# A fused adaLN block on one core: output weights padded by the host, one double tile for the copied heads, the quad's turn two units behind its addition, and other filler rates

## The chip, the cores and the metric

The kernel runs on one core of a Trainium2 chip. The metric is the device time of one execution in microseconds (us). Times are compared as medians over runs; a profiled execution gives one further time and the trace behind every row shown here. The engines are called PE (matrix products), ACT, DVE, POOL and SP; SP issues nearly all DMAs, in its program's order.

## The reference

One transformer block over x of 2048 rows by 448 columns, in float32 (16 heads of 28 columns, a causal sliding window of 256):

```python
mod = (_silu(c) @ w_mod).reshape(c.shape[0], 6, 1, -1)
sa, ca, ga, sb, cb, gb = ...
h = _layernorm(x) * (1 + ca) + sa
x = x + ga * attention(h, wqkv, wo)      # softmax(q k^T * 28**-0.5, window 256) v, then @ wo
h = _layernorm(x) * (1 + cb) + sb
x = x + gb * (mish(h @ w1 + b1) @ w2)    # w1: 448 x 1792, w2: 1792 x 448
```

## The kernel before

**Precision.** Each float32 factor is split into a high part (rounded to the type that PE takes at full rate) and a low part, the difference. A product is made of three passes (high-high, high-low, low-high). For the probabilities, ACT writes the exponential twice (`P` exact, line 733, `Ph` rounded, line 734), and POOL subtracts them (`Pl`, line 741).

**Stages.** The 2048 rows form four groups of 512. A start-up stage normalises group 0 and makes its first projections. Then comes the attention loop, and behind it the two products with w1 and w2 (the feed-forward part, lines 938 and 1124 to 1126), in which PE alone decides.

**The attention loop.** It runs over 64 *slots* (group, head), each of three *units*; u counts units, 48 to a group, and v = u - 48 g is a unit's number within its group. All engines work through their own instructions in the order in which the loop wrote them. In a unit the loop writes, in this order:

- `PV(u-4, Pl)`, the product of low probabilities and values; in the first unit of a slot, `EV` copies a finished head out of PSUM on ACT (line 757);
- `B(u)`: the score product (line 719) and mask (line 730) on PE, then the two exponentials;
- `SP(u-1)`: the subtraction on POOL;
- `A`: three slots ahead, a score product (line 689) whose row maximum DVE takes (line 691). Two PSUM banks serve these;
- in every second slot `M2`: the maxima of two heads are transposed on PE into a corner of the last of those banks (line 697), DVE reads it out as `mr` (lines 699 and 700), and SP copies `mr` into two extra rows of the query tiles (`q<-mr`), so that `B` subtracts the maximum by itself. `B` of those heads waits for that copy; the next but one `A` product waits for DVE to have read the corner, since it reuses the bank;
- the steps of the *quad* (below), a share of *filler*, and `PV(u-2, Ph)`.

**The quad.** `EV` leaves a head as 60 rows in `O2`: 32 of high part (28 of output, one of denominator, three of zero), then 28 of low part. A single `O2` tile has room for two heads, one in either half. `EM`, one unit later, copies both parts with two DMAs into four-head tiles `O4` and `OL4` (`o<-t` with 32 rows, `ol<-t` with 28 rows). When four heads are there, four steps follow in four units, from u = 20 + 12 qd on: `QA` adds the tiles on POOL (line 777), `T1` transposes 32x32 blocks on DVE and takes the reciprocal of the denominators (lines 783, 785), `TM` multiplies on POOL (line 790), `T2` transposes back on DVE (line 794). After the fourth quad a group's attention output is full.

**Filler.** In between, PE makes the products that other groups need: in group g the last query and key tiles of g (`qk_5`, `qk_2`, `qk_6`), then, once the output of group g-1 is full, the products with wo of group g-1 (`wo`), then transposes and projections of group g+1 (`tr`, `qk`, `qk_v`). `RATE[g]` credits are added per unit, `FRONT[g]` units at double rate, and pieces are taken while credit lasts. `load_slot` forces what a coming slot needs, so that in unit 34 of a group a large piece runs at once. A side generator loads and prepares weights; its DMAs stand in a list `later` and are issued one at a time.

**wo.** In group 0 the side generator loads wo: four tiles `wop`, each zeroed on POOL (line 575) and filled by four DMAs of 28 rows (`wo_load`, four heads of 28 rows at a spacing of 32). It then multiplies them by the gate and splits them.

Of the kernel before, what the change touches and what calls it, by code (L numbers as in the profile page):

```python
# [51 lines left out]
def adaln_block(ctx: ExitStack, tc: tile.TileContext, x, wqkv, wo, w1, b1, w2, c, w_mod, out):  # L52
    nc = tc.nc
    PE, ACT, DVE, POOL = nc.tensor, nc.scalar, nc.vector, nc.gpsimd
# [3 lines left out]
    def dma(o, i):  # L58
        nc.sync.dma_start(o, i)

    def pool(name, side="left", space=None):
        kw = {} if space is None else {"space": space}
        cm = tc.tile_pool(name=name, bufs=1, reuse_waits="tile", side=side, **kw)
        st = ExitStack()
        return st.enter_context(cm), st
# [25 lines left out]
    def bank(tag, bufs, name):  # L91
        return PS[0].tile([128, 512], F32, name=name, tag=tag, bufs=bufs)
# [18 lines left out]
    for k in range(4):  # L111
        wmf = st0.tile([128, 2 * D], F32, name=f"wm01_{k}")
        t = wmf[0:112]
# [217 lines left out]
    later = []  # L331
# [190 lines left out]
    att, att_s = pool("att")  # L522
# [1 line left out]
    Q3 = [Q2[i // 2][:, i % 2] for i in range(NQ)]  # L524
    k3_tile(att, NK - 1)

    O4, OL4, (T4, O2) = [[att.tile([128, GT], F32, name=f"{n}_{i}") for i in range(2)] for n in ("o4", "ol4", "t4")]
    for t in OL4:
        POOL.memset(t, 0.0)
    wo3 = [mid.tile([128, D], F32R, name=f"wo3_{i}", tag="wo", bufs=8) for i in range(4)]  # L530
    wol = [mid.tile([128, D], F32R, name=f"wol_{i}", tag="wo", bufs=8) for i in range(4)]

# [11 lines left out]
    def gen_wm_sum(i, pl):  # L544
        ws = []
        for k in range(4):
            wm_load(i, k, pl, ws)
            yield
        yield
        yield  # L550
        flush()
        for k in range(4):
            yield "dve"
            mod_sum(k, ws[k], ws[0])
        yield
        return ws[0]

    def gen_mod_wo():
        acc = yield from gen_wm_sum(2, qk)
        yield "bank"  # L560
        p = bank("mm", 2, "ga")
        PE.matmul(p[:, 0:D], ones, acc, start=True, stop=True)
        ga = xr_tile("ga")[:, 0:D]
        ACT.activation(ga, p[:, 0:D], AF.Copy)
        pieces = []

        def wo_load(ci, t):
            for a in range(4):
                r = (4 * ci + a) * DH
                dma(t[32 * a:32 * a + DH], wo[r:r + DH, :])  # L570

        for ci in range(4):
            t = stg(qk, f"wop{ci}")
            pieces.append(t)
            POOL.memset(t, 0.0)
            later.append(lambda ci=ci, t=t: wo_load(ci, t))
            yield
        yield
        flush()
        for ci in range(4):  # L580
            w = pieces[ci]
            POOL.tensor_tensor(w, w, ga, op=ALU.mult)
            yield "act"
            split_hi(w, wo3[ci], ACT)
            yield "dve"
            split_lo(w, wo3[ci], wol[ci], 0, DVE)
            yield
# [87 lines left out]
    NS = NG * H  # L675
    mx, Pt, Ph, Pl, pvb = {}, {}, {}, {}, {}
# [59 lines left out]
    def SP(u):  # L736
        i, b = divmod(u, 3)
        c0 = units(i // H, b)[0][3]
        Pl[u] = att.tile([128, 512], F32R, name=f"Pl{u}", tag="Pl", bufs=4)
        for eng, a, b in ((POOL, c0, 512),) if u < NU - 5 else ((POOL, 0, 256), (DVE, 256, 512)):  # L740
            eng.tensor_tensor(Pl[u][:, a:b], Pt[u][:, a:b], Ph[u][:, a:b].bitcast(F32), op=ALU.subtract)  # L741
# [12 lines left out]
    def EV(i):  # L754
        a, b, n = i % 4 * 32, i % 2 * 64, i // 4 % 2
        if i < NS - 4:
            ACT.activation(O2[b:b + 60], pvb[i][0:60, :], AF.Copy)
        else:
            ACT.activation(O4[n][a:a + 32], pvb[i][0:32, :], AF.Copy)
            DVE.tensor_copy(OL4[n][a:a + DH], pvb[i][32:60, :])  # L760

    def EM(i):
        a, b, n = i % 4 * 32, i % 2 * 64, i // 4 % 2
        if i < NS - 4:
            dma(O4[n][a:a + 32], O2[b:b + 32])
            dma(OL4[n][a:a + DH], O2[b + 32:b + 60])

    def quad(qd):
        g, ci = divmod(qd, 4)
# [4 lines left out]
    def QA(qd):  # L774
        o, t = quad(qd)
        for eng, a, b in ((POOL, 0, GT),) if qd < NS // 4 - 1 else ((POOL, 0, 192), (DVE, 192, GT)):
            eng.tensor_tensor(o[:, a:b], O4[qd % 2][:, a:b], OL4[qd % 2][:, a:b], op=ALU.add)

    rcq = {}

# [221 lines left out]
            told[g] = next(side[g], None)  # L1002

    RATE = {0: 0.62, 1: 0.97, 2: 0.97, 3: 0.65}
    FRONT = {0: 0, 1: 2, 2: 2, 3: 2}
    ln1 = {g: gen_ln1(g) for g in range(1, NG)}
    fillers = {g: fill_main(g) for g in range(NG)}
# [2 lines left out]
    def step(g):  # L1010
        return next(fillers[g], 99.0) or RATE[g]

# [29 lines left out]
    for i in range(LEAD):  # L1042
# [4 lines left out]
        if i % 2:  # L1047
            M2(i // 2, "A")
            load_slot(LEAD + 1)
    NU = 3 * NS  # L1050
    credit = 0.0
    for u in range(NU + 9):
        s, k = divmod(u, 3)
        g = s // H
        if k == 0 and s % H == 0 and 0 < g < NG:
            drain(fillers[g - 1], side[g - 1])
            flush()
        pipe.step()
        if 0 <= u - 4 < NU:
            PV(u - 4, Pl)  # L1060
            if k == 0:
                EV(s - 2)
        if u < NU:
            B(u)
        if 0 <= u - 1 < NU:
            SP(u - 1)
        a = s + LEAD
        if a < NS:
            A(a, (0, 1, 3)[k])
        if k == s % 2 and s < NS:  # L1070
            load_slot(s + LEAD + 2)
        qd, w = divmod(u - 20, 12)
        if 0 <= qd < NS // 4 - 1 and w < 4:
            (QA, T1, TM, T2)[w](qd)
        if k == 0 and s - 2 == NS - 1:
            for f in (QA, T1, TM, T2):
                f(NS // 4 - 1)
        if g < NG:
            v = u - 48 * g
            if v in (0, 12):  # L1080
                chunk["v"] = 4 if v == 0 and g or 0 < g < NG - 1 else 2
            if v == 0:
                credit = 0.0
            credit += RATE[g] * (2 if v < FRONT[g] else 1)
            while credit > 0.0:
                credit -= step(g)
        if k == 0 and (a - 1) % 2 == 1 and LEAD <= a - 1 < NS:
            M2((a - 1) // 2)
        if g < NG:
            if v > 1 or g == 0:  # L1090
                side_step(g, ("dve", "act")[a >= NS:] if k == 1 else ("act",) if k == 0 and s % 2 == 0 else ())
            if later and ((s + (k == 2)) % 2 == 0 or k == 1):
                later.pop(0)()
        if k == 1 and 0 <= s - 2:
# [65 lines left out]
    for n in range(NN + 1):  # L1160
        g, f = divmod(n, NF)
# [44 lines left out]
```

## Time and profile before

| quantity | value |
|---|---|
| median of 3 runs (lowest, highest) | 742.61 us (738.5, 749.46) |
| the profiled execution | 740.08 us, its span 738.3 us |
| PE busy | 690.1 us, 93% of the span |
| DVE, ACT, POOL busy | 395.3, 391.5, 348.6 us |
| mean granted clock of PE | 0.98 |
| chain that ended last | PE 30%, of it most in lines 938 and 1124 to 1126 |

The page takes the span from the first to the last instruction; 1.8 us of the execution lie outside it. The attention loop's first exponential starts at 47.8 us and its last group at 347.8 us; from about 450 us on PE is busy without a break. Rows of a timeline give start, duration, engine, line and operation, and in square brackets how long the engine stood idle before and what ended that. "PEclk" is the clock that PE was granted, 1.00 being full speed.

### The profile page before, as it was taken

The page shows a single profiled execution, that of the slowest core. Times are in us where ns is not written, and L with a number is a line of the kernel's source. Part 1 is how long each engine was busy: PE and PEld are TensorE (multiplying, and loading weights), DVE is VectorE, ACT ScalarE, POOL GpSimd, SP SyncE. Part 2 cuts the span into 40 slices and gives each one's busy share as a digit, 9 for nine tenths or more (in the row PEclk, how much of TensorE's full clock was granted, in tenths as well). Part 3 has the DMA queues.
Part 4 walks back from the last instruction along what each step waited for, and adds up shares of the span by engine and source line. Part 5 has one row for each costly group of instructions (what it writes and reads, how often), then busy time and mean ns, then how long its engine had stood idle before and what let it go on. Part 6 is the DMA issues. An engine that isn't in the chain of part 4 may idle for free. (4 is left out here: it accounts for less than half of the span.)

```text
span 738.3 us, 12000 instructions
## 1 busy us (share of the span) xinstructions
PE 690.1 (93%) x3873; PEld 585.9 (79%) x3873; DVE 395.3 (54%) x993; ACT 391.5 (53%) x723; POOL 348.6 (47%) x364
## 2 busy tenths in 40 slices
PE   8999888889999979999979789999999999999996
PEld 7777667668887858888768678888888888888885
DVE  5677654667856677846658886333323232413112
ACT  4568565568846677856767795334224223322221
POOL 6536585678656688737678967432010000000002
PEclk9999998989999999999999999999999999999999
DMA  7856764265566374485676338410200020001001
GB/s 215 263 189 208 223 187 144 63 203 158 168 187 203 109 217 148 120 233 160 195 223 186 92 87 273 135 38 0 101 1 1 0 100 1 0 1 51 0 1 50
DMA packets 53730, 91.13 MB, mean 123 GB/s; under 512 B 8086, under 2 KB 28228, under 8 KB 53668
## 3 DMA queue, kind: packets, MB, share of 16 engines
q1 hardware_dynamic: 53204, 90.36, 40.0%
q8 instruction: 31, 0.51, 0.3%
q14 instruction: 31, 0.25, 0.1%
q10 hardware_dynamic: 464, 0.00, 0.0%
HBM read 53.34 MB, written 29.36 MB: 112 GB/s over the span
## 5 line engine op out<-in xcount | busy, mean ns | idle before, releaser
L741 POOL TENSOR_TENSOR Pl<-P,Ph 128x512 fp32r<-128x512 f32 (+2 forms) x192 | 232.3, 1217 | 105.7 <-ACT Ph L734 69.2
L691 DVE CUSTOM_DVE_ANT_0 junk<-sA,mask 128x384 bf16<-128x384 f32 (+2 forms) x256 | 135.2, 528 | 104.2 <-PE sA L689 93.0
L733 ACT ACTIVATE P<-sB 128x512 f32<-128x512 f32 (+2 forms) x192 | 109.6, 571 | 81.8 <-PE sB L730 74.8
L946 DVE TENSOR_TENSOR al<-t,ah 128x512 fp32r<-128x512 f32 x56 | 40.0, 714 | 187.3 <-ACT ah L945 187.3
L944 ACT ACTIVATE t<-z,b1c 128x512 f32<-128x512 f32 x56 | 38.5, 687 | 188.9 <-PE z L938 185.7
L689 PE MATMUL sA<-k,q 84*128 84x384 f32 (+2 forms) x256 | 103.4, 408 | 19.8 <-DVE mr L700 10.5
L734 ACT ACTIVATE Ph<-sB 128x512 fp32r<-128x512 f32 (+2 forms) x192 | 109.4, 570 | 0.0
L719 PE MATMUL sB<-q,k 86*128 86x256 f32 (+1 forms) x352 | 77.7, 295 | 16.1 <-DMA q<-mr 13.5
L938 PE MATMUL z<-hhf,w 128*128 128x512 f32 x224 | 89.5, 399 | 0.0
L938 PE MATMUL z<-hlf,w 128*128 128x512 f32 x224 | 88.5, 395 | 0.0
L1124 PE MATMUL acc<-w2h,ah 128*128 128x448 f32 x224 | 81.9, 366 | 0.0
L1126 PE MATMUL acc<-w2h,al 128*128 128x448 f32 x224 | 81.8, 365 | 0.0
L1125 PE MATMUL acc<-w2l,ah 128*128 128x448 f32 x224 | 81.6, 364 | 0.0
L751 PE MATMUL pv<-Ph,v 128*60 128x256 f32 (+2 forms) x352 | 79.8, 302 | 0.0
L719 PEld LDWEIGHTS sB<-q,k 86*128 86x128 f32 x352 | 62.1, 195 | 21.4 <-issue 10.8
L751 PE MATMUL pv<-Pl,v 128*60 128x256 f32 (+2 forms) x352 | 75.6, 289 | 0.1
L689 PEld LDWEIGHTS sA<-k,q 84*128 84x128 f32 x256 | 50.4, 199 | 30.5 <-DVE mx L691 14.1
L938 PE MATMUL z<-hhf,w1l 128*128 128x512 f32 x168 | 66.4, 395 | 0.0
L730 PE MATMUL sB<-fdmask,identr 128*128 128x128 bf16 (+1 forms) x320 | 61.6, 259 | 0.0
L751 PEld LDWEIGHTS pv<-Ph,v 128*60 128x60 f32 x352 | 47.2, 137 | 12.9 <-issue 0.6
L1133 POOL TENSOR_TENSOR yo<-yo,x 128x448 f32<-128x448 f32 (+1 forms) x4 | 4.2, 1058 | 108.1 <-DVE yo L1130 108.1
L751 PEld LDWEIGHTS pv<-Pl,v 128*60 128x60 f32 x352 | 47.1, 136 | 7.8 <-POOL Pl L741 0.4
(157 smaller groups left out, 1289.3 us busy)
## 6 DMA issues: line engine op xcount, KB each, us to landing
scr<-st SPq DMA_DIRECT2D x24, 512.0 KB
k<-scr SPq DMA_DIRECT2D x48, 252.0 KB
q<-scr SPq DMA_DIRECT2D x64, 168.0 KB
scr<-st SPq DMA_DIRECT2D x32, 256.0 KB
x<-x1d SPq DMA_DIRECT2D x10, 448.0 KB
o<-t SPq DMA_DIRECT2D x60, 64.0 KB
xin<-in_A_x_dram SPq DMA_DIRECT2D x8, 448.0 KB
xr<-in_A_x_dram SPq DMA_DIRECT2D x16, 224.0 KB
```

The lines of the kernel that those rows point to most:

```text
L689: PE.matmul(p[:, c0:384], q[0:84, t * 128:(t + 1) * 128], k[0:84, t * 128 + c0:t * 128 + 384], start=True, stop=True)
L691: DVE.tensor_tensor_reduce(out=junk[:, c0:384], in0=p[:, c0:384], in1=mask[:, c0:384], scale=1.0, scalar=-3.0e38, op0=ALU.add, op1=ALU.max ...
L719: PE.matmul(p[:, c:c + 128 * (t1 - t0)], k[:, jj * 128:(jj + 1) * 128], q[:, t0 * 128:t1 * 128], start=(n == 0), stop=False, skip_group_ch ...
L730: PE.matmul(p[:, c:c + n], identr, fdmask[:, m:m + n], start=False, stop=True, skip_group_check=True)
L733: ACT.activation(P[:, c0:], p[:, c0:], AF.Exp, scale=SCALE)
L734: ACT.activation(Ph[u][:, c0:], p[:, c0:], AF.Exp, scale=SCALE)
L741: eng.tensor_tensor(Pl[u][:, a:b], Pt[u][:, a:b], Ph[u][:, a:b].bitcast(F32), op=ALU.subtract)
L751: PE.matmul(pv[0:60, t0 * 128:t1 * 128], V[j % NV][:, h, :], P[u][:, c:c + 128 * (t1 - t0)], start=(P is Ph and b == 0 and n == 0), stop=F ...
L938: PE.matmul(zb[n], ps[m][1], ps[m][0], start=(m == 0), stop=(m == 10))
L1124: PE.matmul(p, ah[n][:, ts], w2h[f], start=(f == 0), stop=False)
L1125: PE.matmul(p, ah[n][:, ts], w2l[f], start=False, stop=False)
L1126: PE.matmul(p, al[n][:, ts], w2h[f], start=False, stop=(f == NF - 1))
```

## The change

- **wo from the host's layout.** The host pads wo from 16 x 28 rows to 16 x 32 rows with zeros. Each of the four tiles is then filled by one DMA of 128 rows; the four zeroing instructions on POOL and 12 of the 16 DMAs are gone.
- **Double tiles.** `O4` and `OL4` become one tile with two halves, `O4[n][:, 0]` and `O4[n][:, 1]`. Both copies of `EM` have 32 rows. `O2` becomes two tiles of two heads each, so that `EV(i)` reuses the place of head i-4 and not of head i-2.
- **The turn.** `QA`, `T1`, `TM` and `T2` stand in units 0, 2, 3 and 5 behind u = 20 + 12 qd, where they stood in 0, 1, 2 and 3.
- **Filler rates.** In the first 13 units of a group (behind `FRONT`) the rate is multiplied by 0.65 in groups 1 and 2 and by 0.8 in group 3; from unit 13 on by 1.15 in groups 1 to 3. Group 0 keeps its rate.

```diff
-    O4, OL4, (T4, O2) = [[att.tile([128, GT], F32, name=f"{n}_{i}") for i in range(2)] for n in ("o4", "ol4", "t4")]
-    for t in OL4:
+    O4 = [att.tile([128, 2, GT], F32, name=f"o4_{i}") for i in range(2)]
+    O2 = [att.tile([128, GT], F32, name=f"o2_{i}") for i in range(2)]
+    T4 = att.tile([128, GT], F32, name="t4")
+    for t in O2:
         POOL.memset(t, 0.0)
+    POOL.memset(O4[(NG * H // 4 - 1) % 2][:, 1], 0.0)
...
-        def wo_load(ci, t):
-            for a in range(4):
-                r = (4 * ci + a) * DH
-                dma(t[32 * a:32 * a + DH], wo[r:r + DH, :])
...
-            POOL.memset(t, 0.0)
-            later.append(lambda ci=ci, t=t: wo_load(ci, t))
+            later.append(lambda ci=ci, t=t: dma(t, wo[ci * 128:(ci + 1) * 128, :]))
...
-            ACT.activation(O2[b:b + 60], pvb[i][0:60, :], AF.Copy)
+            ACT.activation(O2[i // 2 % 2][b:b + 60], pvb[i][0:60, :], AF.Copy)
...
-            dma(O4[n][a:a + 32], O2[b:b + 32])
-            dma(OL4[n][a:a + DH], O2[b + 32:b + 60])
+            for j in range(2):
+                dma(O4[n][a:a + 32, j], O2[i // 2 % 2][b + 32 * j:b + 32 * j + 32])
...
+    LATE = {0: 1.0, 1: 1.15, 2: 1.15, 3: 1.15}
+    EARLY = {0: 1.0, 1: 0.65, 2: 0.65, 3: 0.8}
...
+    QSTEP = {0: QA, 2: T1, 3: TM, 5: T2}
...
-        if 0 <= qd < NS // 4 - 1 and w < 4:
-            (QA, T1, TM, T2)[w](qd)
+        if 0 <= qd < NS // 4 - 1 and w in QSTEP:
+            QSTEP[w](qd)
...
-            credit += RATE[g] * (2 if v < FRONT[g] else 1)
+            credit += RATE[g] * (2 if v < FRONT[g] else EARLY[g] if v < 13 else LATE[g])
...
+        if name == "A_wo":
+            a = _np.pad(a.reshape(H, DH, D), ((0, 0), (0, 32 - DH), (0, 0))).reshape(H * 32, D)
```

**DVE around the eighth quad's first transposition** (group 2, unit 9; `t` and `on` are the quad's tiles, `mr` the maxima read out, `junk,mx` a row maximum). Before:

```order
L691 ISA junk,mx_3551<-sA_0_3552,mask 128x384
L691 ISA mx_3551 128x1
L783 STREAM_TRANSPOSE t_0_466<-on_2426 128x512
L785 RECIPROCAL rc_3556<-t_0_466 128x16
L699 CAST mr_3559<-sA_3_3530 8x128
L700 TENSOR_TENSOR mr_3559<-sA_3_3530,mr_3559 8x128
L691 ISA junk,mx_3551<-sA_1_3578,mask 128x384
```

and now:

```order
L688 ISA junk,mx_3535<-sA_0_3536,mask 128x384
L688 ISA mx_3535 128x1
L696 CAST mr_3540<-sA_3_3514 8x128
L697 TENSOR_TENSOR mr_3540<-sA_3_3514,mr_3540 8x128
L688 ISA junk,mx_3535<-sA_1_3559,mask 128x384
L688 ISA mx_3535 128x1
L780 STREAM_TRANSPOSE t_466<-on_2404 128x512
L782 RECIPROCAL rc_3565<-t_466 128x16
```

The transposition and the reciprocal, which wait for `QA` on POOL, stood ahead of the two instructions that read the maxima out; they now stand behind these and behind one more row maximum. The same holds at every quad of the loop.

**SP in group 0, where wo is loaded** (`wop` are the tiles of wo, `scr<-st` a store of projected queries and keys, `q<-mr` the copy of the maxima). Before:

```order
L59 DMA wop_1361<-in_A_wo_dram 28x448 x4
L59 DMA wop_1393<-in_A_wo_dram 28x448 x4
L59 DMA o_0_462<-t_1_467 32x512
L59 DMA ol_0_464<-t_1_467 28x512
L59 DMA wop_1423<-in_A_wo_dram 28x448 x4
L59 DMA scr<-st_1_1392 128x2x512
L59 DMA scr<-st_1_1392 128x512
L59 DMA q_0_376<-mr_1511 1x8x128 x2
```

and now:

```order
L59 DMA wop_1360<-in_A_wo_dram 128x448
L59 DMA wop_1388<-in_A_wo_dram 128x448
L59 DMA o_0_462<-o_0_464 32x512 x2
L59 DMA wop_1417<-in_A_wo_dram 128x448
L59 DMA scr<-st_1_1387 128x2x512
L59 DMA scr<-st_1_1387 128x512
L59 DMA q_0_376<-mr_1492 1x8x128 x2
```

Ahead of this `q<-mr` stand nine DMAs fewer in these rows; three more are gone at the first `wop` tile, a few rows earlier. Both copies of a head now have 32 rows.

**PE's filler**, counted unit by unit in PE's order (too long to show): in groups 1 and 2 the tile `qk_6` ends in unit 5 before and in unit 6 now, and the products with wo start in unit 16 before and in unit 18 now, so that the run of units without filler is 6 to 15 before (ten) and 7 to 17 now (eleven). At a group's end it is 46 and 47 before and 45 to 47 now (with four transposed columns in one of them). The forced piece in unit 34 has 33 products before and 26 now. In group 3, `qk_6` ends in unit 8 before and in 10 now, and wo starts in 16 before and in 17 now, and ends in 30 in both. Group 0 is the same in both.

More of the change, by code (lines that the diff above doesn't have):

```diff
@@ L756, in EV @@
         if i < NS - 4:
-            ACT.activation(O2[b:b + 60], pvb[i][0:60, :], AF.Copy)
+            ACT.activation(O2[i // 2 % 2][b:b + 60], pvb[i][0:60, :], AF.Copy)
         else:
-            ACT.activation(O4[n][a:a + 32], pvb[i][0:32, :], AF.Copy)
-            DVE.tensor_copy(OL4[n][a:a + DH], pvb[i][32:60, :])
+            ACT.activation(O4[n][a:a + 32, 0], pvb[i][0:32, :], AF.Copy)
+            DVE.tensor_copy(O4[n][a:a + DH, 1], pvb[i][32:60, :])
     def EM(i):
@@ L776, in QA @@
         for eng, a, b in ((POOL, 0, GT),) if qd < NS // 4 - 1 else ((POOL, 0, 192), (DVE, 192, GT)):
-            eng.tensor_tensor(o[:, a:b], O4[qd % 2][:, a:b], OL4[qd % 2][:, a:b], op=ALU.add)
+            eng.tensor_tensor(o[:, a:b], O4[qd % 2][:, 0, a:b], O4[qd % 2][:, 1, a:b], op=ALU.add)
     rcq = {}
@@ L1196 @@
     for name in _INS:
-        a = _np.ascontiguousarray(inputs[name])
+        a = inputs[name]
+        if name == "A_wo":
+            a = _np.pad(a.reshape(H, DH, D), ((0, 0), (0, 32 - DH), (0, 0))).reshape(H * 32, D)
+        a = _np.ascontiguousarray(a)
         arrays[f"in_{name}_dram"] = a
```

## The prediction

> **What bounds the kernel now.** I began with the page: its busy line and, of the slices, PE and its clock (tenths of each fortieth of the span).
>
> ```profile
> PE 690.1 (93%) x3873; PEld 585.9 (79%) x3873; DVE 395.3 (54%) x993; ACT 391.5 (53%) x723; POOL 348.6 (47%) x364
> PE   8999888889999979999979789999999999999996
> PEclk9999998989999999999999999999999999999999
> ```
>
> The second half of the span, the feed-forward part, is full on PE, and no edit touches it. PE's gaps lie in the attention loop, some 50 to 450 us. Next I asked who waited for whom, in the loop's terms (us in all, times, longest).
>
> ```profile
> PE sB L719 <- DMA q<-mr: 13.5, 7, 5.7
> PE sA L689 <- DVE mr L700: 10.5, 7, 3.0
> PE sA L689 <- DVE mx L691: 8.2, 16, 1.1
> PE sB L719 <- ACT Ph L734: 2.3, 3, 1.3
> ACT t L757 <- DMA ol<-t: 11.1, 8, 3.0
> DVE t L783 <- POOL on L777: 6.1, 5, 2.1
> ```
>
> Both large PE waits are for the maxima: `sA` for their being read out of its bank, `sB` for their copy landing. DVE's wait for POOL (`t <- on`, T1 waiting for QA) is not PE's own, but what is queued behind T1 is that very read-out. The timeline shows it, DVE and PE in group 2:
>
> ```profile
> 262.87 0.08 DVE L691 DVE_READ_ACCUMULATOR2_ANT mx<- 128x1 f32 x1
> 265.08 0.71 DVE L783 STREAM_TRANSPOSE t<-on 128x512 f32<-128x512 f32 x1 [2.13 <-POOL on L777]
> 265.83 0.25 DVE L785 RECIPROCAL rc<-t 128x16 f32<-128x16 f32 x1
> 266.25 0.28 DVE L700 TENSOR_TENSOR mr<-sA,mr 8x128 fp32r<-8x128 f32 x1
> 266.58 0.45 PE L689 MATMUL sA<-k,q 84*128 84x384 f32 x1 [2.96 <-DVE mr L700]
> ...
> 158.39 0.71 DVE L783 STREAM_TRANSPOSE t<-on 128x512 f32<-128x512 f32 x1 [2.11 <-POOL on L777]
> 159.88 0.69 PE L689 MATMUL sA<-k,q 84*128 84x384 f32 x1 [2.94 <-DVE mr L700]
> ```
>
> DVE stood 2.1 us for QA, spent 1 us on the turn, then freed the bank. The same happens in group 1, at the same unit 9. The largest wait, 5.7 us, is for `q<-mr`; SP's queue before it:
>
> ```profile
> 101.98 3.43 SPq L59 DMA_DIRECT2D wop<-in_A_wo_dram  x8
> 105.51 0.56 SPq L59 DMA_DIRECT2D o<-t  x1
> 106.12 0.81 SPq L59 DMA_DIRECT2D ol<-t  x1
> 107.03 1.78 SPq L59 DMA_DIRECT2D wop<-in_A_wo_dram  x4
> 108.90 0.91 SPq L59 DMA_DIRECT2D scr<-st  x2
> 109.91 1.40 SPq L59 DMA_DIRECT2D q<-mr  x2
> ...
> 104.20 0.28 DVE L700 TENSOR_TENSOR mr<-sA,mr 8x128 fp32r<-8x128 f32 x1
> 112.84 0.66 PE L719 MATMUL sB<-q,k 86*128 86x384 f32 x1 [5.70 <-DMA q<-mr]
> ```
>
> The maxima were ready at 104.48 and issued at 109.91, behind twelve loads of wo. Last, stretches (length; busy and count of PE, weight load, DVE, ACT, POOL; granted clock; DMA share, GB/s): the two stalls, what follows each, the units without filler in groups 1 and 2 (units 6 to 15), and ten units with filler.
>
> ```profile
> 107.20:112.80 5.60, 0.00 (x0) 0.00 (x0) 1.76 (x2) 0.59 (x1) 2.74 (x3) 0.81 0.59 199
> 112.80:117.50 4.70, 4.66 (x17) 3.85 (x18) 0.74 (x5) 2.05 (x5) 1.73 (x2) 0.50 0.73 220
> 267.70:271.10 3.40, 3.40 (x18) 2.91 (x16) 1.96 (x8) 3.04 (x6) 3.36 (x4) 0.51 0.54 139
> 152.30:173.00 20.70, 16.25 (x97) 12.76 (x95) 14.33 (x41) 15.49 (x30) 16.90 (x19) 0.84 0.69 210
> 258.10:278.80 20.70, 16.31 (x104) 12.82 (x102) 15.33 (x43) 16.43 (x33) 17.45 (x20) 0.92 0.72 213
> 278.80:297.40 18.60, 18.60 (x127) 16.75 (x125) 12.70 (x40) 12.21 (x24) 15.23 (x14) 1.00 0.51 158
> ```
>
> With filler PE is full and decides. Without it nobody is full; POOL comes nearest. After each stall the clock is half for a few microseconds, which counts where PE decides.
>
> **The change part by part.** The sum is made against the profiled execution's 740.1 us, 2.5 under the median of 742.6.
>
> *Loads of wo.* Twelve of the sixteen issues go. By the rows above one takes 3.43/8 = 0.43 us, so the nine that stood in these rows give 3.9 us back; the three at the first tile, some 6 us earlier in an equally unbroken queue, give 1.3. What a load of 128 rows takes to issue no row shows; nearest are the gate's loads of 112 rows, and the copies of a head:
>
> ```profile
> L59 SPq DMA_DIRECT2D wm<-in_w_mod_dram x21: 363/432/1877, 1.8 to 349.3; - x21
> L59 SPq DMA_DIRECT2D o<-t x60: 548/564/1374, 59.1 to 425.9; - x60
> L59 SPq DMA_DIRECT2D ol<-t x60: 763/806/1448, 59.9 to 426.5; - x60
> L575 POOL MEMSET wop<- x4: 468/471/477, 93.4 to 98.8; 128x448 f32 x4
> ```
>
> So 0.43 as well (min/median/max in ns). `ol<-t` with 32 rows should cost `o<-t`'s 0.56, a quarter less than its 0.81. Then `q<-mr` is issued 5.4 us earlier, at 104.5, just when the maxima are there. It landed 112.84 - 109.91 = 2.9 us after its issue; so at 107.4, where PE began to wait at 112.84 - 5.70 = 107.14. Of the stall 0.3 stays: 5.4 gained. The half clock behind it costs half of 4.7 us, 2.35; it goes too. Together 7.75; I take 7. The low end is 3, if the landing and not the issue is what is late (the loads still bring their bytes, at a DMA share of 0.59 to 0.73). That a half clock follows is seen after 3.0 us of idleness (267.70: 0.51) as after 5.6. The Trainium skill (TensorE: Matmul & The Clock Gate, What's actually happening) puts the condition at an idle window of about 3.4 us; by that rule 2.35 would go as soon as the stall falls under 3.4, by the row only below 3. The row decides here; my 7 holds under both.
>
> *The turn.* T1 and the reciprocal leave the place ahead of the read-out: 10.5 us of PE waits can go at most. Of these 2.94 + 2.96 lie in the stretches without filler. There POOL limits what can come: 20.70 - 16.90 = 3.8 and 20.70 - 17.45 = 3.25 are all that POOL's own work leaves, so the two stalls fit, barely, 5.9 (low end 0, if POOL cannot run behind by the few buffers it has). The half clock there I count at nothing, since PE is not full. Of the remaining 4.6 I take 3.5. What is late next: T1 now stands ahead of a later maximum, for which PE's `sA` waits too. If it held PE at all 15 quads, that would be 15 x 0.96 = 14.4 us; but it stood ahead of maxima before as well, and two units cover QA (POOL: one subtraction and QA, some 2.5 us of about 4). I take 1. Net: 8.4 gained. T2, two units later than before, waits for nothing more; a group's output is full two units later, which is the filler's matter.
>
> *Two tiles for `O2`.* The 11.1 us that ACT waited go almost surely: its copy now waits for a DMA four heads back. What of it reaches PE is bounded by PE's wait for ACT, 2.3, and by 0 below; the 3.0 falls beside PE waiting for `q<-mr`, where nothing is gained. I take 1.5; the high end is 4, if the stretches without filler gain by it. The shorter second copy (0.24 x 60) is SP's time, counted above where it matters, elsewhere nothing: SP has room. Zeroing: four times 0.47 of POOL goes, one zeroing of similar size is added before the loop, where nobody waits for POOL; nothing.
>
> *Filler.* The same products, elsewhere. Groups 1 and 2 get eleven units without filler instead of ten and three instead of two at the end; group 3 one more: five in all. A unit without filler takes POOL 17.45/10 = 1.75 us. Its own PE work: ten units with filler take 18.60, 1.86 each, of which 4.4 products with wo by the order; a product of that size every 0.21 us by the starts of these two,
>
> ```profile
> 105.96 0.37 PE L323 MATMUL qk_v<-wq,hl 128*128 128x448 f32 x1
> 106.17 0.36 PE L323 MATMUL qk_v<-wq,hh 128*128 128x448 f32 x1
> ```
>
> leaves 0.94. So each costs up to 0.81, 4.0 in all. Low end: what PE idled in the stretch beside the stall, (20.70 - 16.31 - 2.96)/10 = 0.14, 0.7 in all. POOL's row is of the very stretch, so nearer the high end: 2.5 lost.
>
> Sum: -7 - 8.4 - 1.5 + 2.5 = -14.4, 725.7, say **726**. With all good ends (7.75, 5.9 + 4.6, 4, 0.7) it is -21.6, 718.5; with modest ones (3; 3.5; 0; 4.0 lost) -2.5, 737.6.
>
> **The rivals.**
>
> *The landing takes the place of the issue.* `q<-mr` waited seven times, 13.5 us, only 5.7 of it behind wo; the rest landed late in busy DMA engines (0.72 in the stretch at 258). Then earlier issues help by half: wo 3.5, the turn 5 (its `sB` waits as long as before), `O2` 0, filler 2.5 lost: -6, **734**. By the skill's 3.4 us, 2 us less, since the halved stall would release the clock. Against it: at 104 to 110 the copy demonstrably stood unissued.
>
> *More goes than counted.* The good ends, and with them the half clocks of the loop: each row at 0.50 lasts 3.4 to 5 us and costs half where PE decides. -21.6 and three of 2: -28, **712**. For it: stalls feed the clock. Against it: POOL's 16.90 and 17.45 of 20.70.
>
> *Slower: the thinner stretch loses the clock.* Units without filler are those in which PE pauses most. If the longer run of them keeps the clock at half throughout (0.84 and 0.92 now), their PE work is 2 x 0.94 = 1.88 us, above POOL's 1.75, and PE sets the pace: eleven take 20.7, as ten do now, so the turn gains nothing there. The five added units cost 1.88 - 0.94 each, 4.7; and each of five stretches ends in a window of 3.4 us at half, in full units, 1.7 each: 8.5. Against that wo's 7 and the turn's 2.5 elsewhere: +3.7, **744**. It decides from a granted clock near 0.5 over units 7 to 17. The Trainium skill's section "HAM oscillation — how this bites in real kernels" on the same page tells of a kernel that falls back to half clock at each wait between short bursts; here the trace has 0.92 and 0.84, so it speaks for it weakly.
>
> That the change does not do what it says is no rival: the order shows all four edits.
>
> **How the numbers follow.** Forecast 0.52 (its own range 718 to 736), landing 0.22, more 0.14, slower 0.10; 0.02 for anything else. The range 711 to 741 leaves out the slower case and the tails. Two per cent of 742.6 is 14.9 us, about what a measurement of this kernel can tell (its three runs span 11): faster means below 727.8. Of the forecast somewhat over half lies there (0.30), and all of "more": 0.44. Slower means above 757, beyond even the slower rival's 744: 0.04, for its tail. Within: 0.52.
>
> **What would show it.** In the changed profile: no `PE <- DMA q<-mr` near 107 us above 1 us; `sA <- mr` under 2 us in all; `DVE t <- POOL on` near 0; `ACT t <- DMA` gone; the second copy at 0.56 us; units 7 to 17 at about 1.75 us each with POOL nearly full. I am wrong if the q<-mr wait remains though its issue is early (landing), if `sA <- mx` grows by what `mr` loses (T1 moved its wait on), or if the clock of units 7 to 17 falls to 0.5.

## The result and the profile after

The changed kernel takes 736.69 us (median of 20 runs, 733.6 to 742.8) against 742.15 us of the kernel before, run beside it on the same chip: a ratio of 0.9928, 95% interval 0.9903 to 0.9954, or about 5.3 us less. The ratios, here and below, are of fast runs alone (a run over 1.5% above the fastest of its kernel is left out), so they need not be the quotients of the medians shown. The forecast was 726, 14.4 less than before's profiled execution. The sign came true, and the time lies inside the range of 711 to 741; the size did not. The profiled execution took 737.18 us, its span 735.4.

The page, busy line and slices of PE and its clock:

```profile
PE 691.6 (94%) x3873; PEld 588.2 (80%) x3873; DVE 400.5 (54%) x993; ACT 392.3 (53%) x723; POOL 347.9 (47%) x361
PE   9899789989999979999889799999999999999996
PEclk9999999999999999999999899999999999999999
```

PE stands idle for 735.4 - 691.6 = 43.8 us, where it was 738.3 - 690.1 = 48.2. But it is also 1.5 us longer busy with the same 3873 products: the idle time fell by 4.4, and a part of that went back to products at half clock. Who waited for whom (us in all, times, longest):

```profile
PE sB L716 <- DMA q<-mr: 10.9, 5, 4.3
PE sA L686 <- DVE mx L688: 5.7, 10, 1.7
PE sB L716 <- ACT Ph L731: 3.1, 6, 0.8
ACT o L754 <- PE pv L748: 15.0, 22, 1.4
PEld sA L686 <- DVE mr L697: 2.6, 9, 0.3
DVE t L780 <- POOL on L774: 1.7, 3, 0.8
```

PE's wait for the read-out (`mr`, 10.5 us before) is gone but for a rest of the weight loads, ACT no longer waits for the copies of a head (`EV` now waits for PE alone), and T1 waits 1.7 us for QA instead of 6.1. Yet the wait for `q<-mr` has only gone from 13.5 to 10.9. The timeline of SP, DVE and PE where wo is loaded:

```profile
102.32 0.90 SPq L59 DMA_DIRECT2D wop<-in_A_wo_dram  x2
103.32 2.13 SPq L59 DMA_DIRECT2D o<-o  x2
105.19 0.28 DVE L697 TENSOR_TENSOR mr<-sA,mr 8x128 fp32r<-8x128 f32 x1
105.50 0.58 SPq L59 DMA_DIRECT2D wop<-in_A_wo_dram  x1
106.18 0.92 SPq L59 DMA_DIRECT2D scr<-st  x2
107.20 1.59 SPq L59 DMA_DIRECT2D q<-mr  x2
111.05 0.41 PE L716 MATMUL sB<-q,k 86*128 86x384 f32 x1 [2.77 <-DMA q<-mr]
```

The maxima were ready at 105.47 and issued 1.73 us later (5.43 before), so the queue is indeed shorter. But the copy then took 3.85 us from its issue to PE's start, where it took 2.93. The stall fell from 5.70 to 2.77 us, not to 0.3. A longer stall, of landing alone, stands earlier (the maxima ready at 79.97, the copy issued at once); before, the wait at this place was 3.02:

```profile
79.69 0.28 DVE L697 TENSOR_TENSOR mr<-sA,mr 8x128 fp32r<-8x128 f32 x1
79.93 1.43 SPq L59 DMA_DIRECT2D q<-mr  x2
87.18 0.44 PE L716 MATMUL sB<-q,k 86*128 86x384 f32 x1 [4.25 <-DMA q<-mr]
```

SP's issues (min/median/max in ns) came out as expected: a load of 128 rows takes 0.43 in the median, little more than the 0.38 of one of 28 rows (the first row, from before), and the second copy of a head, now of 32 rows, costs 0.58 instead of 0.81:

```profile
L59 SPq DMA_DIRECT2D wop<-in_A_wo_dram x16: 330/383/496, 96.3 to 108.4; - x16
L59 SPq DMA_DIRECT2D o<-o x120: 508/582/1575, 60.1 to 424.5; - x120
L59 SPq DMA_DIRECT2D wop<-in_A_wo_dram x4: 371/428/582, 97.6 to 105.5; - x4
```

Stretches: the stall, what follows it, and the units without filler, 7 to 17 of groups 1 and 2 (from exponential to exponential):

```profile
107.20:111.00 3.80, 1.07 (x7) 0.67 (x5) 2.23 (x6) 1.45 (x3) 3.80 (x5) 1.00 0.91 291
111.30:114.70 3.40, 3.40 (x14) 2.91 (x14) 1.00 (x5) 1.84 (x5) 1.57 (x3) 0.51 0.91 224
147.00:168.10 21.10, 17.13 (x109) 13.52 (x108) 15.03 (x42) 18.42 (x35) 19.17 (x21) 0.92 0.74 222
251.90:272.40 20.50, 15.82 (x104) 12.54 (x103) 15.43 (x39) 18.21 (x34) 18.30 (x21) 0.92 0.65 201
```

Half clock still follows. In the stall the DMA engines are busy to 0.91. What the copy landed among is told by the packets that began between its issue and PE's start, first before, then now ("under 2 KB" counts those under 512 B too; the second row of each gives packets, MB and the share of the engines' time):

```profile
DMA packets 476, 0.85 MB, mean 291 GB/s; under 512 B 48, under 2 KB 64, under 8 KB 476
q1 hardware_dynamic: 476, 0.85, 76.2%
DMA packets 635, 1.11 MB, mean 289 GB/s; under 512 B 67, under 2 KB 195, under 8 KB 635
q1 hardware_dynamic: 635, 1.11, 91.4%
```

In both, most packets (412 and 440) have 2 KB or more, as a row of 512 float32 in the stores `scr<-st` has; two of these stores stand right ahead of `q<-mr` in either queue. New are 112 rows of wo (1792 bytes each, all that lies between 512 B and 2 KB but the copy's own 16 packets; their load was issued only 1.7 us earlier). The engines are busy to 0.91 where they were busy to 0.76 over this time. The later landing thus goes with a fuller stretch, in which wo is the smaller part.

The units without filler take 21.1/11 = 1.92 and 20.5/11 = 1.86 us, where they took 2.17 (21.7 for the ten of group 1) and 2.07, and where the forecast had 1.75. By the starts of the units' exponentials in the two traces the change is 5.9 us ahead at unit 2 of group 1, some 6 at the start of group 3, and 3.0 at that group's unit 47. This pair of profiles differs by 2.9 us in its spans, less than the medians do.

### The profile page after: what moved, and what is told of

Read it like the earlier page. It is cut to its first block, busy times and chain, and to the rows that moved or that the text cites. A ratio compares the mean times of both kernels' runs of the same rounds, so it can differ in the third digit from the quotient of the medians.

```text
span 735.4 us, 11954 instructions
## 1 busy us (share of the span) xinstructions
PE 691.6 (94%) x3873; PEld 588.2 (80%) x3873; DVE 400.5 (54%) x993; ACT 392.3 (53%) x723; POOL 347.9 (47%) x361
## 3 DMA queue, kind: packets, MB, share of 16 engines
q1 hardware_dynamic: 53468, 90.97, 40.8%
## 5 line engine op out<-in xcount | busy, mean ns | idle before, releaser
L716 PE MATMUL sB<-q,k 86*128 86x256 f32 (+1 forms) x352 | 77.3, 294 | 15.3 <-DMA q<-mr 10.9
```

What stands on the lines that cost most here:

```text
L716: PE.matmul(p[:, c:c + 128 * (t1 - t0)], k[:, jj * 128:(jj + 1) * 128], q[:, t0 * 128:t1 * 128], start=(n == 0), stop=False, skip_group_ch ...
```

## The experiments

Differences in us are the ratio's distance from 1 times the time of before that was run beside it (742.8 to 743.6).

### Each part alone

`e1_wo` is the kernel before with the loads of wo of the change, and nothing else:

```diff
-            POOL.memset(t, 0.0)
-            later.append(lambda ci=ci, t=t: wo_load(ci, t))
+            later.append(lambda ci=ci, t=t: dma(t, wo[ci * 128:(ci + 1) * 128, :]))
```

> The kernel before with the padded wo alone (twelve DMA issues and four zeroings fewer, nothing else). Theory A, the gains are real and the filler gives them back: the stall at unit 36 of group 0 falls from 5.7 to about 2.7 us, 3 to 5 us faster in all. Theory B, no single edit is worth more than 2 us because a landing or POOL follows right behind each wait: 0 to 2 us faster, the stall moved to the next copy of the maxima.

Measured: 738.01 us, ratio 0.9943 (0.9913 to 0.9972), -4.2. DVE, SP and PE in its timeline, then PE's largest wait for the copy:

```profile
102.12 0.28 DVE L694 TENSOR_TENSOR mr<-sA,mr 8x128 fp32r<-8x128 f32 x1
103.61 1.86 SPq L59 DMA_DIRECT2D q<-mr  x2
108.26 0.41 PE L713 MATMUL sB<-q,k 86*128 86x384 f32 x1 [3.20 <-DMA q<-mr]
```

```profile
PE sB L713 <- DMA q<-mr: 9.1, 9, 3.2
```

Issued 1.2 us after the maxima, landed 4.65 us after the issue: the landing took over a part of what the queue gave back.

`e2_turn` is before with the turn of the change alone:

```diff
-        if 0 <= qd < NS // 4 - 1 and w < 4:
-            (QA, T1, TM, T2)[w](qd)
+        if 0 <= qd < NS // 4 - 1 and w in QSTEP:      # {0: QA, 2: T1, 3: TM, 5: T2}
+            QSTEP[w](qd)
```

> The kernel before with the turn alone (T1, TM, T2 in units 2, 3 and 5). Theory A: the waits of the score product for the maxima's read-out all but go (10.5 to under 2 us) and units 8 to 12 of groups 1 and 2 become 3 us shorter each, 6 to 9 us faster in all. Theory B: POOL is next in these units and takes it back within the group, 0 to 2 us faster.

Measured: 742.58 us, ratio 0.9975 (0.9944 to 1.0006), -1.9. Waits of PE, then DVE, SP and PE at the loads of wo:

```profile
PE sB L719 <- DMA q<-mr: 18.6, 10, 6.7
PE sA L689 <- DVE mx L691: 4.6, 9, 0.9
PEld sA L689 <- DVE mr L700: 2.7, 9, 0.3
PE qk L323 <- DVE hl L270: 2.9, 2, 1.5
```

```profile
101.07 0.28 DVE L700 TENSOR_TENSOR mr<-sA,mr 8x128 fp32r<-8x128 f32 x1
107.92 1.39 SPq L59 DMA_DIRECT2D q<-mr  x2
110.83 0.66 PE L719 MATMUL sB<-q,k 86*128 86x384 f32 x1 [6.68 <-DMA q<-mr]
```

The wait for the read-out is gone, and that for the copy has grown by 5.1. At the loads of wo the maxima come 3.1 us earlier than before and are issued 2.0 earlier, so they stand 1.1 longer in SP's queue; that accounts for 1.0 of the 5.1, and the rest, at other heads, was not taken apart. The filler's `qk` waits 2.9 us for the low part of its input (0.6 before), the transposition of the maxima 2.6 for the last of them (0.8), and `PV` 1.6 for POOL (none). In all PE stands idle 46.9 us in this profile, only 1.3 less than before, though its execution (737.20 us) is among the shortest of the twelve: most of what the read-out gave back is waited for elsewhere. And with T2 two units later the filler itself moves: in PE's order the products with wo begin in unit 18 instead of 16, so that units 6 to 17, twelve of them, are without filler.

`e3_filler` is before with the new rates alone, `e4_tiles` with the double tiles alone:

```diff
-            credit += RATE[g] * (2 if v < FRONT[g] else 1)                                      # e3
+            credit += RATE[g] * (2 if v < FRONT[g] else EARLY[g] if v < 13 else LATE[g])
...
-            ACT.activation(O2[b:b + 60], pvb[i][0:60, :], AF.Copy)                              # e4
+            ACT.activation(O2[i // 2 % 2][b:b + 60], pvb[i][0:60, :], AF.Copy)
...
-            dma(O4[n][a:a + 32], O2[b:b + 32])
-            dma(OL4[n][a:a + DH], O2[b + 32:b + 60])
+            for j in range(2):
+                dma(O4[n][a:a + 32, j], O2[i // 2 % 2][b + 32 * j:b + 32 * j + 32])
```

> The kernel before with the filler rates alone (the output of a group is still full at unit 11). Theory A: the longer run without filler costs 2 to 3.5 us in each of groups 1 and 2, and some 2 in group 3: 4 to 9 us slower. Theory B: the same products at another time, within 2 us of before.

> The kernel before with the double tiles alone (O4 with two halves, two O2 tiles, both copies of 32 rows). Both theories: ACT's waits for the copies go (11.1 us to under 1). Theory A: 0 to 2 us faster, since PE waited for other things at the same time. Theory B: 0, and SP's wait for earlier stores grows instead.

Measured: `e3_filler` 747.33 us, ratio 1.0045 (1.0017 to 1.0074), +3.3; `e4_tiles` 742.06 us, ratio 0.9971 (0.9943 to 0.9999), -2.1, ACT's waits for the copies gone, PE's much as before. The four parts add to -4.9, against -5.3 for the whole: within their intervals, of some 2 us to either side each, the parts add up, and the gap to the forecast lies in them.

### Without the rates; the copy from another queue; POOL relieved

`e5_no_filler` is the change at the old rates. `e6_mr_act` is e5 with `q<-mr` issued by ACT, where no load stands ahead of it. `e7_split` is e5 with the subtraction of units 6 to 17 of groups 1 to 3 shared between POOL (352 columns) and DVE (160). `e8_both` has both.

```diff
-            credit += RATE[g] * (2 if v < FRONT[g] else EARLY[g] if v < 13 else LATE[g])
+            credit += RATE[g] * (2 if v < FRONT[g] else 1)                      # e5 to e8
...
-            dma(Q2[pr % (NQ // 2)][84 + i:85 + i].bitcast(F32)...
+            nc.scalar.dma_start(Q2[pr % (NQ // 2)][84 + i:85 + i].bitcast(F32)...  # e6, e8
...
+        light = u // 48 > 0 and 6 <= u % 48 <= 17
+        for eng, a, b in ((POOL, 0, 352), (DVE, 352, 512)) if light else ...    # e7, e8
```

> The changed kernel with the filler rates of before: padded wo, double tiles and turn alone. The single edits gave 4.2, 1.9 and 2.1 us as ratios of 0.9943, 0.9975 and 0.9971. Theory A, they add up: 0.987 to 0.991, some 8 us faster than before and 3 faster than the changed kernel. Theory B, they share one gain (each removes the same waits behind SP's queue): 0.992 to 0.995, no better than the padded wo alone or the changed kernel.

> e5_no_filler with the copy of the maxima issued from ACT's queue instead of SP's. If the copies are late because they stand behind other issues in SP's queue, the score product's waits for them fall to a half or less and the time by 3 to 6 us below e5_no_filler. If they are late in the DMA engines, the waits stay and the time is within 1.5 us of it. If ACT, which now waits for DVE before each copy, holds its exponentials up, it is 3 us or more slower.

> e5_no_filler with the subtraction of units 6 to 17 in groups 1 to 3 split between POOL (352 columns) and DVE (160). If POOL's work is what holds the units without filler (the reason that the turn gave 1.9 us and not 8), they become 1 to 2.5 us shorter in each group and the time falls by 3 to 6 us. If it is ACT or the copies of the maxima, nothing moves (within 1.5 us), or DVE's extra work makes it slower.

> e5_no_filler with both, the copies of the maxima from ACT's queue and the split subtraction. If both causes are real and separate, 6 to 10 us below e5_no_filler; if one of them is the next limit behind the other, more than the sum of the two single gains; if neither is, within 1.5 us.

Measured:

| kernel | median us | ratio (95%) | us |
|---|---|---|---|
| e5_no_filler | 736.63 | 0.9895 (0.9852 to 0.9939) | -7.8 |
| e6_mr_act | 745.61 | 1.0038 (1.0015 to 1.0060) | +2.8 |
| e7_split | 736.22 | 0.9909 (0.9874 to 0.9944) | -6.8 |
| e8_both | 744.69 | 1.0024 (0.9999 to 1.0050) | +1.8 |

PE's waits for ACT and for the copy, in e6 and then in e5:

```profile
PE sB L716 <- DMA q<-mr: 8.9, 5, 3.9
PE sB L716 <- ACT Ph L731: 7.8, 8, 3.0
PEld sB L716 <- ACT Ph L731: 14.0, 15, 3.2
```

```profile
PE sB L716 <- DMA q<-mr: 12.3, 7, 4.5
PEld sB L716 <- ACT Ph L731: 2.6, 5, 1.1
```

With no load ahead of it the copy is still waited for 8.9 us: that much is not owed to SP's queue. At each of these five waits the copy was issued as soon as the maxima were there, and PE started 3.7 to 6.3 us after the issue, so they are landings. What is gained (3.4) is lost on ACT, whose exponentials now stand behind the issues, each of which waits there for its maxima: e6 is some 10 us slower than e5 (+2.8 against -7.8), and e8 does no better. Relieving POOL moves nothing that these intervals show. The sums of units 6 to 17 in groups 1 to 3, of e5 and then of e7:

```profile
sum 68.36, PE 51.99 PEld 40.64 DVE 52.06 ACT 56.26 POOL 59.33; mean PE 17.33 PEld 13.55 DVE 17.35 ACT 18.75 POOL 19.78
sum 66.06, PE 53.70 PEld 42.53 DVE 62.27 ACT 56.24 POOL 47.85; mean PE 17.90 PEld 14.18 DVE 20.75 ACT 18.75 POOL 15.95
```

POOL has 11.5 us less to do, and the units are 2.3 us shorter. So the split does not show that POOL sets their pace, full as it looks there. It does not rule it out either: DVE has 10.2 us more to do, is now the fullest engine, and may have taken POOL's place.

### The turn, taken apart

`e10_t1_alone` is before with T1 written at the end of its old unit, behind the read-out; T2 stays, and PE's order is that of before. `e12_hold` is before with its old turn, but the filler is held until unit 13 is reached, which gives PE the order of e2. `e9_t1_late` is e5 with the turn of e10.

```diff
+    QSTEP = {0: QA, 2: TM, 3: T2}                              # e10, e9
...
+        if w == 1 and 0 <= qd < NS // 4 - 1:
+            T1(qd)
...
-            while g - 1 not in on_full:
+            while g - 1 not in on_full or now["v"] < 13:       # e12
```

> The kernel before; T1 stays in its unit but is written behind the reading-out of the maxima, TM and T2 stay where they were, so the filler keeps its place. If the turn of the change gave only 1.9 us because its later T2 delays the products with wo by two units, this is 5 to 7 us faster than before (0.990 to 0.993), the waits for the read-out gone as in e2_turn. If the earlier read-out itself is worth little, since something else holds the units without filler, it is 0 to 2.5 us faster, like e2_turn.

> The kernel before with one thing added: the filler is told two units later that a group's output is full, which gives PE exactly the order that the turn of the change gives it (wo from unit 18, twelve units without filler), while T1, TM and T2 stay. If the late output is the price that ate the turn's gain: 3 to 5 us slower. If not: within 1.5 us of before.

> e5_no_filler (padded wo, double tiles) with the turn of e10_t1_alone in place of that of the change. If the late output is the price: 3 to 5 us faster than e5_no_filler, 0.983 to 0.986 of before. If not: within 1.5 us of e5_no_filler.

Measured: `e10_t1_alone` 742.79 us, ratio 0.9990 (0.9961 to 1.0019), -0.7; `e12_hold` 754.89 us, ratio 1.0172 (1.0136 to 1.0208), +12.8; `e9_t1_late` 737.75 us, ratio 0.9917 (0.9881 to 0.9953), -6.2. Waits of e10, then of e12:

```profile
PE sA L689 <- DVE mx L691: 16.1, 22, 2.4
DVE t L783 <- POOL on L777: 3.9, 3, 1.7
```

```profile
PE sA L689 <- DVE mr L700: 8.6, 5, 3.0
PE sB L719 <- DMA q<-mr: 15.2, 8, 5.9
```

In e10 no read-out is waited for, but the row maxima behind T1 are, 16.1 us instead of 8.2: T1 handed on its wait for QA. In e12 the later start of wo alone, with the old turn, costs 12.8 us, far above either expectation; with the new turn the same order of PE is at -1.9 (e2). So in that order the turn is worth 14.6. By the starts of the exponentials, e12 loses nothing in the units left bare (6 to 17 of groups 1 to 3 take 71.1 us, and 71.3 before, where units 16 and 17 had filler) and 10.6 us in units 18 to 46 behind them, where the postponed products have to go. But neither e10 nor e9 gains from an output that is as early as before: e10 is at -0.7, and e9 is no faster than e5. Both have another turn than the change, one that hands its wait on to the maxima; a turn that waits for nothing and is not late was not built. So how much of the turn's gain went to the order, and how much to other waits, is not separated.

### The place of the filler

`e11_spread` is e9, and `e13_spread_turn` is e5, with one line more: in groups 1 and 2 the rate is 0.4 of itself in units 2 to 10. By PE's order the last products of `qk_2` and those of `qk_6` then stand in units 3, 5, 7 and 9, three or four in each, and the run without filler is units 10 to 17 in e13 (7 to 17 in the change).

```diff
+            credit += RATE[g] * (2 if v < FRONT[g] else 0.4 if 0 < g < 3 and v < 11 else 1)
```

`e14_early` and `e15_late` are before with the lower rate of the first 13 units, or the higher rate behind them, alone. `e16_no_g3_rates` is the change with group 3 at its old rate; `e17_g3_rates` is e13 with group 3 at the change's rates.

> e9_t1_late with the first filler of groups 1 and 2 spread to unit 9 (rate 0.4 from unit 2 to 10, full rate after), so that six units have none instead of ten. If units without filler are PE time lost at some 0.5 us each, 2 to 4 us faster than e9_t1_late. If they are held by ACT and POOL alike, whose work these products add to, within 1.5 us of it or slower.

> The change without its filler rates (about -7.8 us against before so far), with the filler of qk_2 and qk_6 spread over units 3 to 9 of groups 1 and 2 (three or four products in units 3, 5, 7 and 9 instead of 3 to 5). The turn is the change's own, so the products with wo begin in unit 18. Theory A (the spread is what makes the best version good, since the thin units have idle time that the spread filler fills at no price): about -11 to -12, ratio 0.984 to 0.986. Theory B (the spread helps only together with the early output, which lets wo begin in unit 16): about -8, ratio 0.988 to 0.991.

> Before, with the lower rate of the first 13 units alone (no higher rate behind them). Both halves of the filler edit together cost 3.3 us. If the lower early rate is the price (one light unit more in groups 1 and 2 and later products with wo in group 3), about +3; if the denser filler from unit 13 on is the price, about 0, between -1 and +1.

> Before, with the higher rate from unit 13 on alone. If the lower early rate is the price of the filler edit, about 0, between -1 and +1; if the denser filler is, about +3. The smaller forced piece in unit 34 of groups 1 and 2 (18 products instead of 33) could also gain a little, -1.

> The change with group 3 at its old rate (0.65 throughout), the new rates only in groups 1 and 2. In the profiled runs the change loses against the version with the spread filler about 3.5 us in each of groups 1, 2 and 3. Theory A (group 3's lower early rate is the price of the filler edit, as the trace of the early rate alone suggests, where group 3 takes 7 us longer than before): about 733, ratio 0.988. Theory B (the price lies in groups 1 and 2): about 736, ratio 0.992 to 0.993, as the change.

> The best version so far (the change with the filler of groups 1 and 2 spread, 731.4 us, ratio 0.983) with the change's rates in group 3 added (0.8 times in the first 13 units, 1.15 times behind them). Theory A (group 3's rates are the price): about 735, ratio 0.988. Theory B (the price lies in groups 1 and 2): about 731, ratio 0.983.

Measured:

| kernel | median us | ratio (95%) | us |
|---|---|---|---|
| e11_spread | 730.51 | 0.9838 (0.9798 to 0.9878) | -12.0 |
| e13_spread_turn | 731.38 | 0.9828 (0.9794 to 0.9862) | -12.8 |
| e14_early | 748.86 | 1.0068 (1.0042 to 1.0095) | +5.1 |
| e15_late | 744.61 | 1.0016 (0.9989 to 1.0042) | +1.2 |
| e16_no_g3_rates | 736.99 | 0.9906 (0.9873 to 0.9940) | -7.0 |
| e17_g3_rates | 731.61 | 0.9840 (0.9801 to 0.9878) | -11.9 |

e11 and e13 beat both kernels. The spread is what makes them good: it gains 5 to 6 with either turn (e5 to e13, e9 to e11). By the starts of the exponentials in e5 and e13, units 6 to 17 of groups 1 and 2, which hold seven products more in each group, take 46.2 us together instead of 44.1; units 0 to 5 take 25.2 instead of 28.9, and units 18 to 46 take 129.0 instead of 132.5. The higher rate alone (e15) is within noise of before. e17 shows that group 3's rates cost nothing measurable beside the spread, so what separates the change from e13 is the filler of groups 1 and 2. The clock shows part of how. The page's busy line of e13 and its units 10 to 17 of group 1, then the same of e14:

```profile
PE 685.9 (94%) x3873; PEld 583.2 (80%) x3873; DVE 394.5 (54%) x993; ACT 392.0 (54%) x723; POOL 347.5 (48%) x361
```

```profile
150.80:166.50 15.70, 11.93 (x81) 9.02 (x80) 12.83 (x32) 14.26 (x27) 14.14 (x15) 1.00 0.74 222
```

```profile
PE 698.4 (93%) x3873; PEld 592.8 (79%) x3873; DVE 395.9 (53%) x993; ACT 392.4 (52%) x723; POOL 349.4 (47%) x364
```

```profile
158.70:177.20 18.50, 15.67 (x83) 12.95 (x84) 11.29 (x33) 14.32 (x28) 15.05 (x14) 0.72 0.68 196
```

Over the whole kernel the same 3873 products keep PE busy 12.5 us longer in e14. Time at half clock, summed from the trace's clock record without the window behind the last product:

| profiled execution | span | PE busy | PE idle | at half clock |
|---|---|---|---|---|
| before | 738.3 | 690.1 | 48.2 | 27.3 |
| after | 735.4 | 691.6 | 43.8 | 30.7 |
| e12_hold | 753.0 | 697.3 | 55.7 | 51.2 |
| e13_spread_turn | 726.9 | 685.9 | 41.0 | 17.1 |
| e14_early | 750.4 | 698.4 | 52.0 | 51.2 |
| e17_g3_rates | 729.7 | 688.9 | 40.8 | 27.3 |

PE's busy time is 685.9 to 698.4 us in the 19 profiled kernels and, less half of the half clock, 671.7 to 680.4: a good part of a difference of busy time is a difference of clock, not all of it. Between after and e13 busy time makes 5.7 us and idle time 2.8. These are single executions. Over all runs the granted clock is 0.977 in the mean for the change, 0.980 for e17, 0.982 for e13 and for e11, and 0.969 for e14. Times their spans, the change loses at most some 4 us more to the clock than e13, of the 7.5 between them, and 2.4 more than e17, of 6.6. So the clock is a part of the spread's gain and not shown to be all of it. e14 leaves something open too: its profile puts 7 us of its loss in group 3, where wo begins two units later with the old turn, as in e12; which part lies in groups 1 and 2 was not separated.

## Why the prediction was right or wrong

| term | forecast | alone, with its interval |
|---|---|---|
| loads of wo | -7 | -4.2 (-6.5 to -2.1) |
| the turn | -8.4 | -1.9 (-4.2 to +0.4) |
| two tiles for `O2` | -1.5 | -2.1 (-4.2 to -0.1) |
| filler | +2.5 | +3.3 (+1.3 to +5.5) |
| sum | -14.4 | -4.9; together -5.3 (-7.2 to -3.4) |

**Loads of wo: mechanism right, size off.** "`q<-mr` is issued 5.4 us earlier, at 104.5, just when the maxima are there" held but for 1.7 us (1.2 in e1): a load and two stores still stood ahead. The landing "2.9 us after its issue; so at 107.4" failed: 3.85, and 4.65 in e1, in DMA engines busy to 0.91 (after) where it had been 0.76. The duration of a landing was carried over from a time with less traffic into one that the change made fuller. That was the low end, and the first rival's mechanism. Of the half clock behind the stall, which was to go, 3.4 us stayed (6.8 us in before's clock record): it followed 2.77 us of idleness. So the bound of 3 that I had read from one stall was none. The rule of the Trainium skill (TensorE: Matmul & The Clock Gate, What's actually happening), an idle window of about 3.4 us, does not describe this place either. With what stayed of the queue, the term lost two fifths (4.2 for 7).

**The turn: the step that failed.** The read-out waits went wholly, as said, and T1's new place did not become the next wait (`sA <- mx` 5.7, below the 8.2 of before). What failed is the size, "Net: 8.4 gained": alone the turn gave 1.9. The step charged T1, the next to be waited for, with 1 us, and everything else behind the read-out with nothing. In e2 the read-out's 10.5 us of waits are gone, and 3.6 of the maxima's; but 5.1 came back at the copy `q<-mr`, 2.3 at the filler's `qk`, 1.8 at the transposition of the maxima and 1.6 at `PV`, and PE's idle time fell by 1.3. Of the 5.9 us counted in the stretches without filler, 0.9 and 0.7 came in e2 (units 6 to 15: 21.7 to 20.8 and 20.7 to 20.0).

The second part of the step is its last sentence, "a group's output is full two units later, which is the filler's matter", together with the price given there, "so each costs up to 0.81". Alone, the turn leaves two more units without filler in each of groups 1 to 3; e12 prices that order, with the old turn, at 12.8, which is 2.1 for each of the six units. The price had been POOL's time less PE's own work, with PE at full clock and no stall: in e12 PE is idle 7.5 us longer than before (55.7 against 48.2) and busy 7.2 longer, with 51.2 us at half clock. How much of the turn's missing 6.5 us is owed to this order, and how much would have gone to other waits in any order, stays open, since e10 and e9, with the early output, gained nothing.

Turn and filler together were forecast at -5.9 and measured -1.9 + 3.3 = +1.4: of the 9.1 that the forecast was too low against -5.3, 7.3 lie here.

**POOL as the bound of these units: not shown.** POOL is busy to 19.17 of 21.10 and 18.30 of 20.50, and ACT to 18.42 and 18.21; taking a third of the subtraction from POOL did not change the time, though it filled DVE instead (e7). The 1.75 us a unit and with it the price of a light unit rested on POOL alone. A high busy share in a chain where several engines hand work on is not yet a bound. (The row of the prediction for group 1, from 152.30 on, begins with unit 7 and holds nine units, not ten; the 1.75 is from the row of group 2, so the sum does not change.)

**Two tiles: right.** ACT's wait for the copies is gone, and 2.1 reached the time, near the 1.5.

**Filler: size right, place not.** +3.3 against 2.5. But it is not the lower rate or the late start by itself: e13 starts wo as late as the change and has its early filler at a still lower rate, and it gains. What separates the two is where the filler of groups 1 and 2 stands.

**The rivals.** *Landing* (734) described the loads of wo and came closest, 2.7 us off. In part this is luck: it put the turn at 5, which gave 1.9, and of the waits it called late landings the one of 2.4 us at 383 had stood 2.15 in SP's queue. *More goes* (712) fell: half clock did not get less in the change (30.7 against 27.3). *Slower* (744) fell for the change, whose units 7 to 17 have a clock of 0.92 and not 0.5. Its mechanism is seen once: 0.72 in group 1 of e14, where time went up by 5.1. The section "HAM oscillation — how this bites in real kernels" of the Trainium skill (TensorE: Matmul & The Clock Gate) tells of such losses at each wait between bursts; in e14 and e12 the trace agrees in part, with 51.2 us at half clock.

**What would show it.** No `q<-mr` wait near 107 above 1 us: 2.77, wrong. `sA <- mr` under 2: for PE none, 2.6 of weight loads. `DVE t <- POOL on` near 0: 1.7. ACT's waits for DMA gone: yes. The second copy at 0.56: 0.58. Units 7 to 17 at 1.75: 1.92 and 1.86. The named condition of failure, a wait that remains though its issue is early, is what came at wo.

## What to carry to other kernels

A step that is moved later moves all that is released by its result; where a planner starts other work on "output full", read the new order and price it, before the wait that is saved (that order alone cost 12.8 us with the old turn). A saved wait is a gain only after the next ones in line are priced too: here 10.5 us went and 1.3 of idle time was gained. A transfer that is issued earlier into fuller DMA engines can land later (3.85 and 4.65 us for 2.93), so its old landing time is no forecast. When PE has too little to do in a stretch, spreading a few products over it in small portions (here three or four every second unit) was worth 5 us, as much as the whole change, for one more line.

## What the runs showed of the hardware that was not expected

*One subtraction on DVE, 0.68 to 2.80 us.* `hlo` in the change (16 alike, min/median/max in ns), then one of them on DVE's timeline with PE's wait behind it, then POOL in that time:

```profile
L629 DVE TENSOR_TENSOR hlo<-on,hho x16: 678/1446/2801, 161.1 to 450.3; 128x512 fp32r<-128x512 f32 x16
```

```profile
265.24 2.80 DVE L629 TENSOR_TENSOR hlo<-on,hho 128x512 fp32r<-128x512 f32 x1
268.57 0.44 PE L686 MATMUL sA<-k,q 84*128 84x384 f32 x1 [1.69 <-DVE mx L688]
```

```profile
264.00:267.00 3.00, 3.00 (x4) 0.84 0.89 243
```

During the long one POOL works without a break (the last row is a stretch with POOL's busy time, clock, DMA share and GB/s). The maximum behind `hlo` came late, and PE waited 1.69 us. The Trainium skill (SBUF — State Buffer, Who interferes with whom) states that a DVE instruction with two inputs in SBUF contends with a POOL instruction that reads SBUF; this pair is of that kind. No run took it apart.

*Issuing from ACT.* The copy's issue takes ACT's queue 0.63 us and SP's 0.64, but ACT's next exponential stands behind it and its wait: 64 of them made e6 some 10 us slower than e5.

*Rows of a DMA.* 128 rows of wo take little longer to issue than 28 did (0.43 against 0.38), while a copy of 28 rows within the chip took longer than one of 32 (0.81 against 0.58).
